# Sinkhorn attention feeding an affine ResMLP on one core: bulk loads placed elsewhere, and the strided weight columns of v copied by GpSimd into tiles of their own

## The chip, the cores and the metric

The kernel runs on one core of one Trainium2 chip. The metric is the device time of one execution in microseconds (us), the median of several runs. A core has TensorE for matmuls (PE in the profile, with its weight loads shown apart as PEld), VectorE (DVE), ScalarE (ACT), GpSimd (POOL) and SyncE (SP). In this kernel SyncE only issues DMAs; GpSimd computes and also issues the DMAs that convert float32 inputs to 16 bits on their way into the core.

## What is computed

The first half is attention over 8 blocks of 96 rows whose keys and values are mixed across blocks by a matrix P, made from `sort_net` by five rounds of exponential, row and column normalisation. The second half is a token mix and a two-layer channel MLP.

```python
# q, k, v: (4, 8, 768, 64); sort_net: (4, 8, 8, 8)
for _ in range(5):
    P = exp(P - max(P, -1)); P = P / (sum(P, -1) + 1e-9); P = P / (sum(P, -2) + 1e-9)
k_sorted, v_sorted = einsum('bhij,bhjcd->bhicd', P, k_b), einsum('bhij,bhjcd->bhicd', P, v_b)
attn = softmax(0.125 * q_b @ k_sorted.T)          # inside each of the 8 blocks of 96
x = (attn @ v_sorted)                              # -> (4, 768, 512), heads side by side
a1 = alpha1 * x + beta1
u = x + lam * einsum('ts,bsd->btd', w_tok, a1)     # w_tok (768, 768)
out = u + lam * (relu((alpha2 * u + beta2) @ w_ch1) @ w_ch2)   # 512 -> 2048 -> 512
```

## The kernel before, in words

The four batches pass through attention, then through a bounce to DRAM that turns the layout round, then through the MLP. The order of the instructions on each engine is the order in which the program is written; the program interleaves generators by hand, and there is no scheduler.

The opening, in order: GpSimd issues the loads of q and k of batch 0, v of batches 0 and 1 (one tile, `raw`), k of batch 1, the token matrix `wt16`, and three broadcasts of `lam`, `alpha1` and `beta1` over 128 partitions (L156 to L158). `sinkhorn(0)` makes P for batches 0 and 1 (L192 to L212). `mix_k01(0)` mixes the keys of batch 0 on TensorE (L277), and ScalarE and VectorE evict each psum tile, half each (`evict_k`, L259 and L261), into two tiles `kT`. Then GpSimd issues `load_q(1)`, all of W1 and W2 and half of the second v load (L142, L668, L670, L128).

`scores_max(0)` (matmuls L399, row maxima L405 on VectorE) runs interleaved with `mix_v01` (L319), which mixes the values of batches 0 and 1. Its weights are columns of `raw` seen as (t, d): the 96 elements of one column stand 64 elements apart. ScalarE evicts most of it (L327).

`heads(0)` runs softmax and values of batch 0 in eight steps (`scores` L443 and L451, exponential L458, `values` L468, scaled L478). After steps 3 and 7, `bounce` writes a half of x to DRAM in six DMAs and reads it back in one (L491, L493, on the SyncE queue); the result is `x16`, in halves g = 0 and 1. Six sums of rows of `wt16` (`row_sum`, L619 on VectorE and L622 on ScalarE) stand between the steps. GpSimd then makes `rb` from them (L696, six instructions) and `add_x(0)` adds `rb` to x (L515), so `u` is started.

While x travels, TensorE transposes `wt16` (`tok_weights`, L607), mixes the keys of batch 1 (`mix_k01(1)`) and transposes q of batch 1 (`q_path(1)`, L366). GpSimd issues the second k load and `load_q(2)` behind `add_x(0)`.

From there two generators are interleaved by credits: `mixing` (token mix `tok_mix`, L525, with L531 on VectorE, the addition L532 on GpSimd and the cast L533 on ScalarE; transposes `u_transposes` L542; channel layers `ch1` L571 and `ch2` L590) and `attention` for the batches 1 to 3. `sinkhorn(1)` is advanced one step at each part of `mixing`. The attention ends long before `mixing` does; the end of the program is the channel layers of batch 3.

Of the kernel before, what the change touches and what calls it, by code (L numbers as in the profile page):

```python
# [19 lines left out]
def kernel(  # L20
# [18 lines left out]
    nc = tc.nc  # L39
# [110 lines left out]
    load_k01(1)  # L150
    wt16 = moep.tile([128, NT, S], F16, name="wt16", tag="u", bufs=2)
    nc.gpsimd.dma_start(wt16[:], moe_w_tok.rearrange("(k p) s -> p k s", p=128))
    lamB = wt([128, C], FT, "lamB")
    b1lB = mt([128, C], FT, "tmp", 2)
    a1lB = wt([128, C], FT, "a1lB")
    nc.gpsimd.dma_start(lamB[:], moe_lam.partition_broadcast(128))  # L156
    nc.gpsimd.dma_start(a1lB[:], moe_alpha1.partition_broadcast(128))
    nc.gpsimd.dma_start(b1lB[:], moe_beta1.partition_broadcast(128))  # L158
# [28 lines left out]
    def sinkhorn(bp):  # L187
# [59 lines left out]
    def kT_tiles(b):  # L247

        for h2 in range(2):
            kT_of[b, h2] = at([128, 16, BLK], F16, "kT", 4)  # L250

    def evict_k(b, ps, cols, t16):
        for h2 in range(2):
            dst = kT_of[b, h2][:, :, t16 * 16:(t16 + 1) * 16].rearrange(
                "p c (b t) -> p c b t", b=2
            )
            src = cols[:, h2 * 16:h2 * 16 + 16]
            if h2 == 0:
                nc.scalar.copy(dst, src)  # L259
            else:  # L260
                nc.vector.tensor_copy(dst, src)  # L261

    def mix_k01(b, pools):
        raw = raw_of["k", 0]
        kT_tiles(b)
        for t16 in range(BLK // 16):
# [15 lines left out]
            evict_k(b, ps, ps[:, :, 0:256].rearrange("p b (t c) -> p c b t", c=32), t16)  # L282
            yield

    def mix_k23(P, pools):
        raw = raw_of["k", 1]
        for b in (2, 3):
            kT_tiles(b)
        for t16 in range(BLK // 16):
# [13 lines left out]
            for b2 in range(2):  # L303
                evict_k(2 + b2, ps, cols[:, b2 * 32:b2 * 32 + 32], t16)
# [8 lines left out]
    def mix_v01(pool):  # L313

        raw = raw_of["v", 0][:].rearrange("p (t d) -> p d t", d=D)
        for d8 in range(D // 8):
            ps = ps2(pool)
            for dd in range(8):
                nc.tensor.matmul(  # L319
                    ps[0:BLK, dd // 4, (dd % 4) * 128:(dd % 4 + 1) * 128],  # L320
                    raw[:, d8 * 8 + dd, :], PV[:], start=True, stop=True,
                )
# [66 lines left out]
    def scores_max(b):  # L389

        mx = at([BLK, 2, H4, NB], FT, "mx", 1)
        for n in range(2 * H4):
            h4, g = divmod(n, 2)
            sp = ps2(psS)
            for i1 in range(4):
                i = g * 4 + i1
                for hl in range(2):
# [4 lines left out]
                        kT_of[b, h4 // 2][r, h4 % 2 * 8 + i, :],  # L402
# [29 lines left out]
    def heads(b, xpool):  # L432
# [5 lines left out]
        def scores(n):  # L438
# [8 lines left out]
            for i1 in range(4):  # L447
                i = g * 4 + i1
                for hl in range(2):
# [3 lines left out]
                        kT_of[b, h4 // 2][r, h4 % 2 * 8 + i, :],  # L453
# [56 lines left out]
    def add_x(b):  # L510
        u_of[b] = mt([128, NT, C], FT, "u", 2)
        for g in range(2):
            for k0, kn in ((0, 2), (2, 1)):
                kt = slice(g * 3 + k0, g * 3 + k0 + kn)
                nc.gpsimd.tensor_tensor(  # L515
                    u_of[b][:, kt], x16_of[b, g][:, k0:k0 + kn], rb[:, kt], ALU.add
                )
# [18 lines left out]
    def u_transposes(b, half):  # L536
        for c2 in range(2):
            ps = psS.tile([128, 2, 1024], BF, name="uT_ps", tag="psS")
# [127 lines left out]
    load_q(1)  # L666
    for ci in range(CT):
        nc.gpsimd.dma_start(W1[:, ci, :], moe_w_ch1[ci * 128:(ci + 1) * 128, :])  # L668
# [120 lines left out]
```

## Time and profile before

| | |
|---|---|
| median of 3 runs | 355.72 us (353.84 to 356.33) |
| profiled execution: its own time, its span | 356.3 us, 354.5 us |
| TensorE busy, weight loads busy | 310.7 us (88%), 187.7 us |
| VectorE, ScalarE, GpSimd busy | 157.0, 123.1, 117.1 us |
| mean granted TensorE clock | 0.968 |
| first matmul of `tok_mix(0)`, first matmul of `ch1` | 68.03 us, 99.08 us |
| last matmul of attention's last stage to the end | 231.7 to 354.5 us: channel layers and token mixes alone |

The span runs from the first to the last instruction. Times inside it are counted from its start. Busy shares are means over stages with different limits: TensorE is busy for nearly all of the time after about 100 us, and has holes before.

### The profile page before, as it was taken

How to read it: one execution, taken by the hardware profiler on the slowest of the kernel's cores; microseconds unless marked ns; L12 is line 12 of the kernel's file. 1: busy time of each engine (PE TensorE's matmuls, PEld its weight loads, DVE VectorE, ACT ScalarE, POOL GpSimd, SP SyncE). 2: the span in 40 equal slices, each digit the busy share in tenths (PEclk: the TensorE clock that was granted, in tenths of full speed). 3: DMA queues.
4: the chain of work that ended last, by engine and by line, in shares of the span. 5: the costliest groups of instructions: out<-in, count | busy, mean ns of one | idle time of the engine just before them, and what ended most of it. 6: DMA issues, size and time to landing. Idle time of an engine off the chain costs nothing.

```text
span 354.5 us, 6763 instructions
## 1 busy us (share of the span) xinstructions
PE 310.7 (88%) x2878; PEld 187.7 (53%) x2878; DVE 157.0 (44%) x298; ACT 123.1 (35%) x204; POOL 117.1 (33%) x113
## 2 busy tenths in 40 slices
PE   1869998666578889999889989999999999999994
PEld 1768888422245544654455645664554554554541
DVE  4355474235654444559644583434311134213223
ACT  3225564202334522642443503533331225240310
POOL 8223573385200011836311001718211657300000
PEclk9999999986868999999999999999999999999998
DMA  7999999549000233697014401301410200100101
GB/s 95 220 203 251 214 211 232 162 90 185 3 0 2 46 84 109 229 152 98 11 59 112 91 2 59 77 2 41 137 46 1 91 0 0 61 30 31 59 16 73
DMA packets 33325, 31.76 MB, mean 90 GB/s; under 512 B 15696, under 2 KB 28752, under 8 KB 32784
## 3 DMA queue, kind: packets, MB, share of 16 engines
q0 software_dynamic: 8912, 15.60, 23.7%
q1 hardware_dynamic: 24384, 15.75, 17.7%
q8 instruction: 22, 0.36, 0.4%
q14 instruction: 7, 0.06, 0.0%
HBM read 35.14 MB, written 11.01 MB: 130 GB/s over the span
## 4 chain that ended last, share of the span: by engine, by line
PE 78%; DVE 6%; ACT 5%; DMA 4%; issue 3%; POOL 2%; SPq 1%; DVEq 0%; ACTq 0%; POOLq 0%
PE psM L571 25%; PE psM L590 23%; PE psM L525 8%; PE psM L319 3%; PE psS L399 3%; PE psS L468 3%; PE psS L443 3%; DMA xscr<-xnat 3%; ACT ET L458 3%; PE psS L451 2%; PE uT_ps L542 2%; PE q_ps L366 1%; PE psM L468 1%; PE psS L297 1%; DVE mx L405 1%
## 5 line engine op out<-in xcount | busy, mean ns | idle before, releaser
L571 PE MATMUL psM<-a2T,W 128*128 128x384 bf16 x512 | 91.6, 334 | 0.0
L590 PE MATMUL psM<-W,hT 128*128 128x512 bf16 x384 | 87.4, 379 | 0.0
L571 PEld LDWEIGHTS <-W 128*128 128x128 bf16 x512 | 49.2, 100 | 32.8 <-issue 2.7
L599 POOL TENSOR_TENSOR u<-u,tmp 128x512 f32<-128x512 f32 x18 | 22.8, 1268 | 124.4 <-DVE tmp L597 67.7
L581 ACT ACTIVATE hT<-psM 128x768 bf16<-128x768 f32 x48 | 38.9, 811 | 70.9 <-PE psM L571 70.9
L590 PEld LDWEIGHTS <-hT 128*128 128x128 bf16 x384 | 36.5, 98 | 41.0
L525 PE MATMUL psM<-x,w_tokT 128*128 128x512 f16 x144 | 37.9, 415 | 2.4 <-DMA x<-xscr 2.4
L532 POOL TENSOR_TENSOR u<-u,tmp 128x512 f32<-128x512 f32 x24 | 30.4, 1272 | 25.1 <-DVE tmp L531 20.9
L458 ACT ACTIVATE ET<-psS 96x768 f16<-96x768 f32 x32 | 25.5, 803 | 35.6 <-PE psS L451 35.6
L597 DVE TENSOR_TENSOR tmp<-psM,lamB 128x512 f32<-128x512 f32 x24 | 16.6, 691 | 47.0 <-PE psM L590 46.1
L579 DVE TENSOR_SCALAR hT<-psM 128x768 bf16<-128x768 f32 x16 | 15.3, 957 | 41.6 <-PE psM L571 41.6
L405 DVE TENSOR_REDUCE mx<-psS 96x8 f32<-96x768 f32 x32 | 29.9, 947 | 7.2 <-PE psS L399 7.1
L533 ACT CAST u<-u 128x512 bf16<-128x512 f32 x24 | 14.8, 618 | 48.2 <-POOL u L532 48.2
L515 POOL TENSOR_TENSOR u<-x,rb 128x1024 f32<-128x1024 f16 (+1 forms) x16 | 25.7, 1638 | 12.0 <-DMA x<-xscr 12.0
L525 PEld LDWEIGHTS <-w_tokT 128*128 128x128 f16 x144 | 13.9, 104 | 19.6 <-issue 6.7
L531 DVE TENSOR_TENSOR tmp<-psM,a1lB 128x512 f32<-128x512 f32 x24 | 16.6, 690 | 14.4 <-PE psM L525 14.4
L468 PEld LDWEIGHTS <-ET 96*96 96x96 f16 x256 | 16.4, 140 | 6.0 <-ACT ET L458 2.1
L201 PE MATMUL psS<-sortP,blk 128*128 128x8 f32 x20 | 4.6, 304 | 14.4 <-DVE sortP L198 9.3
L142 POOL DMA_DIRECT2D qn<-in_q_dram x16 | 11.6, 739 | 16.3 <-DMA raw<-in_v_dram 6.7
L478 DVE TENSOR_TENSOR xnat<-psS,recip 96x512 f16<-96x512 f32 x24 | 16.5, 686 | 1.2 <-DVE recip L477 0.3
L399 PEld LDWEIGHTS <-qT 64*96 64x96 f16 x256 | 10.2, 147 | 11.4 <-issue 9.3
L399 PE MATMUL psS<-kT,qT 64*96 64x96 f16 x256 | 13.6, 242 | 2.9 <-DVE mx L405 1.5
(96 smaller groups left out, 310.8 us busy)
## 6 DMA issues: line engine op xcount, KB each, us to landing
out_dram<-u SPq DMA_DIRECT2D x24, 256.0 KB, 2.0
W<-in_moe_w_ch_dram POOLq DMA_DIRECT2D x8, 512.0 KB, 14.3
qn<-in_q_dram POOLq DMA_DIRECT2D x16, 192.0 KB, 8.2
raw<-in_k_dram POOLq DMA_DIRECT2D x8, 384.0 KB, 8.2
xscr<-xnat SPq DMA_DIRECT2D x48, 64.0 KB, 2.2
x<-xscr SPq DMA_DIRECT2D x8, 384.0 KB, 3.3
raw<-in_v_dram POOLq DMA_DIRECT2D x1, 1536.0 KB, 16.2
raw<-in_v_dram POOLq DMA_DIRECT2D x4, 384.0 KB, 20.3
```

Of the source, the lines that this page charges most:

```text
L399: nc.tensor.matmul(sp[0:BLK, hl, i1 * BLK:(i1 + 1) * BLK], qT_of[b, h4][r, i * BLK:(i + 1) * BLK], kT_of[b, h4 // 2][r, h4 % 2 * 8 + i, :] ...
L405: nc.vector.tensor_reduce(mx[:, :, h4, g * 4:(g + 1) * 4], sp[0:BLK, :, 0:4 * BLK].rearrange("p l (i t) -> p l i t", t=BLK), AXX, ALU.max,)
L458: nc.scalar.activation(ET[:].rearrange("p l i s -> p l (i s)"), sp[0:BLK, :, 0:4 * BLK], AF.Exp, scale=scale,)
L468: nc.tensor.matmul(xp[0:BLK, hl, i1 * VP:i1 * VP + D + 1], ETs[n][:, hl, i1, :], vS[:, (hl * H4 + h4) * 8 + g * 4 + i1, 0:D + 1], start=Tr ...
L515: nc.gpsimd.tensor_tensor(u_of[b][:, kt], x16_of[b, g][:, k0:k0 + kn], rb[:, kt], ALU.add)
L525: nc.tensor.matmul(ps[:, 0, :], w_tokT[ks][:, kt * 128:(kt + 1) * 128], x16_of[b, ks // 3][:, ks % 3, :], start=(ks == 0), stop=(ks == NT ...
L531: nc.vector.tensor_tensor(tmp[:], ps[:, 0, :], a1lB[:], ALU.mult)
L532: nc.gpsimd.tensor_tensor(u[:, kt], u[:, kt], tmp[:], ALU.add)
L571: nc.tensor.matmul(ps[:, m1, 0:384], W1[:, ci, m * 128:(m + 1) * 128], a2T_of[b, half, ci][:], start=(ci == 0), stop=(ci == CT - 1),)
L581: nc.scalar.activation(t_[:], ps[:, :, 0:384], AF.Relu)
L590: nc.tensor.matmul(ps[:, 0, :], hT[m // 2][:, m % 2, k1 * 128:(k1 + 1) * 128], W2[:, m, :], start=(m == 0), stop=(m == HT - 1),)
L599: eng.tensor_tensor(u[:, kt], u[:, kt], tmp[:], ALU.add)
```

## The change

GpSimd's load order is another: `wt16` comes before k of batch 1, q of batch 1 is issued at the start, only half of W1 is issued before the value mix, the other half after the first half of `add_x(0)`, W2 after its second half, and the second loads of v and k and `load_q(2)` after `tok_mix(0)`. `lam`, `alpha1` and `beta1` are loaded by SyncE into one partition, multiplied there and spread by GpSimd's `partition_broadcast`; the built program has a reload of GpSimd's instruction library before the first of these and another before the first `rb`. `gather` copies eight columns of v at a time (128 x 8 x 96, 16 bits) into a contiguous tile on GpSimd, two ahead of the matmuls that take their weights from it. Each key eviction is one instruction, on ScalarE and VectorE in turn. All row sums are VectorE's and stand beside the value mix. `tok_weights` and `mix_k01(1)` each carry six steps of `sinkhorn(1)`, and `q_path(1)` moves into the interleaved attention. The first row maximum of a Sinkhorn run enters the exponential as a bias. The first `u_transposes` uses the other psum pool.

```diff
...
     load_q(0)
     load_k01(0)
     load_v0()
-    load_k01(1)
     wt16 = moep.tile([128, NT, S], F16, name="wt16", tag="u", bufs=2)
     nc.gpsimd.dma_start(wt16[:], moe_w_tok.rearrange("(k p) s -> p k s", p=128))
+    load_k01(1)
+    load_q(1)
+
+
+    rows = moep.tile([1, 3, C], FT, name="rows", tag="u16", bufs=1)
+    for n, src in enumerate((moe_lam, moe_alpha1, moe_beta1)):
+        nc.sync.dma_start(rows[:, n, :], src.unsqueeze(0))
     lamB = wt([128, C], FT, "lamB")
+    a1lB = wt([128, C], FT, "a1lB")
     b1lB = mt([128, C], FT, "tmp", 2)
-    a1lB = wt([128, C], FT, "a1lB")
-    nc.gpsimd.dma_start(lamB[:], moe_lam.partition_broadcast(128))
-    nc.gpsimd.dma_start(a1lB[:], moe_alpha1.partition_broadcast(128))
-    nc.gpsimd.dma_start(b1lB[:], moe_beta1.partition_broadcast(128))
+    for n in (1, 2):
+        nc.gpsimd.tensor_tensor(rows[:, n, :], rows[:, n, :], rows[:, 0, :], ALU.mult)
+    for n, t_ in enumerate((lamB, a1lB, b1lB)):
+        nc.gpsimd.partition_broadcast(t_[:], rows[:, n, :])
 
     w_tokT = [wt([128, S], F16, f"w_tokT_{i}") for i in range(NT)]
     W1 = wt([128, CT, HID], BF, "W1")
...
         rs = wt([128, 1], FT, f"rs{bp}")
         c8 = wt([128, NB], FT, f"c8{bp}")
 
-        nc.vector.tensor_reduce(rs[:], P[:], AXX, ALU.max)
-        nc.vector.tensor_scalar(P[:], P[:], rs[:], None, op0=ALU.subtract)
+        top = wt([128, 1], FT, f"top{bp}")
+        nc.vector.tensor_reduce(top[:], P[:], AXX, ALU.max, negate=True)
         for it in range(5):
-            nc.scalar.activation(P[:], P[:], AF.Exp, accum_out=rs[:])
+            if it == 0:
+                nc.scalar.activation(P[:], P[:], AF.Exp, bias=top[:], accum_out=rs[:])
+            else:
+                nc.scalar.activation(P[:], P[:], AF.Exp, accum_out=rs[:])
             yield
             nc.vector.reciprocal(rs[:], rs[:])
             nc.vector.tensor_scalar(P[:], P[:], rs[:], None, op0=ALU.mult)
...
 
     kT_of, vS_of = {}, {}
 
-    def kT_tiles(b):
-
-        for h2 in range(2):
-            kT_of[b, h2] = at([128, 16, BLK], F16, "kT", 4)
-
-    def evict_k(b, ps, cols, t16):
-        for h2 in range(2):
-            dst = kT_of[b, h2][:, :, t16 * 16:(t16 + 1) * 16].rearrange(
-                "p c (b t) -> p c b t", b=2
-            )
-            src = cols[:, h2 * 16:h2 * 16 + 16]
-            if h2 == 0:
-                nc.scalar.copy(dst, src)
-            else:
-                nc.vector.tensor_copy(dst, src)
+    def kT_tile(b):
+
+        kT_of[b] = at([128, H4 * NB, BLK], F16, "kT", 2)
+
+    def evict_k(b, cols, t16):
+        dst = kT_of[b][:, :, t16 * 16:(t16 + 1) * 16].rearrange("p c (b t) -> p c b t", b=2)
+        if t16 % 2 == 0:
+            nc.scalar.copy(dst, cols)
+        else:
+            nc.vector.tensor_copy(dst, cols)
 
     def mix_k01(b, pools):
         raw = raw_of["k", 0]
-        kT_tiles(b)
+        kT_tile(b)
         for t16 in range(BLK // 16):
             ps = ps2(pools[t16 % len(pools)])
             for turn in range(2):
...
     def mix_v01(pool):
 
         raw = raw_of["v", 0][:].rearrange("p (t d) -> p d t", d=D)
+        cols = {}
+
+        def gather(d8):
+            cols[d8] = moep.tile([128, 8, BLK], F16, name="vcol", tag="hT", bufs=11)
+            nc.gpsimd.tensor_copy(cols[d8][:], raw[:, d8 * 8:(d8 + 1) * 8, :])
+
+        gather(0)
+        gather(1)
         for d8 in range(D // 8):
+            if d8 + 2 < D // 8:
+                gather(d8 + 2)
             ps = ps2(pool)
             for dd in range(8):
                 nc.tensor.matmul(
                     ps[0:BLK, dd // 4, (dd % 4) * 128:(dd % 4 + 1) * 128],
-                    raw[:, d8 * 8 + dd, :], PV[:], start=True, stop=True,
+                    cols[d8][:, dd, :], PV[:], start=True, stop=True,
                 )
             for b in range(2):
                 dst = vS_of[b][:, :, d8 * 8:(d8 + 1) * 8].rearrange("p c (b d) -> p c b d", b=2)
...
 
     u_of, u16_of, a2T_of = {}, {}, {}
 
-    def add_x(b):
-        u_of[b] = mt([128, NT, C], FT, "u", 2)
-        for g in range(2):
-            for k0, kn in ((0, 2), (2, 1)):
-                kt = slice(g * 3 + k0, g * 3 + k0 + kn)
-                nc.gpsimd.tensor_tensor(
-                    u_of[b][:, kt], x16_of[b, g][:, k0:k0 + kn], rb[:, kt], ALU.add
-                )
+    def add_x(b, g):
+        if g == 0:
+            u_of[b] = mt([128, NT, C], FT, "u", 2)
+        for k0, kn in ((0, 2), (2, 1)):
+            kt = slice(g * 3 + k0, g * 3 + k0 + kn)
+            nc.gpsimd.tensor_tensor(
+                u_of[b][:, kt], x16_of[b, g][:, k0:k0 + kn], rb[:, kt], ALU.add
+            )
 
     def tok_mix(b):
         u = u_of[b]
...
             yield
 
     def row_sum(tt):
-        if tt % 2:
-            nc.vector.tensor_reduce(rowsum[:, tt:tt + 1], wt16[:, tt, :], AXX, ALU.add)
-        else:
-            junk = mt([128, 2, 384], BF, "hT", 11)
-            nc.scalar.activation(
-                junk[:].rearrange("p a c -> p (a c)"), wt16[:, tt, :], AF.Identity,
-                accum_out=rowsum[:, tt:tt + 1],
-            )
+        nc.vector.tensor_reduce(rowsum[:, tt:tt + 1], wt16[:, tt, :], AXX, ALU.add)
+
+    def load_w1(ci):
+        nc.gpsimd.dma_start(W1[:, ci, :], moe_w_ch1[ci * 128:(ci + 1) * 128, :])
 
     def run(gen, n=None):
         while n is None or n > 0:
...
         run(mix, 1)
     run(mix)
 
-    load_q(1)
-    for ci in range(CT):
-        nc.gpsimd.dma_start(W1[:, ci, :], moe_w_ch1[ci * 128:(ci + 1) * 128, :])
+    for ci in range(CT // 2):
+        load_w1(ci)
+    top, mix = scores_max(0), mix_v01(psM)
+    run(top, 3)
+    for n in range(5):
+        run(mix, 1)
+        run(top, 1)
+        if n > 1:
+            row_sum(n - 2)
+    run(mix, 1)
+    run(top, 1)
+    row_sum(3)
+    run(mix, 1)
+    run(top)
+    row_sum(4)
+    run(mix)
+
+    att0 = heads(0, psM)
+    run(att0, 2)
+    row_sum(5)
+    run(att0)
+    for tt in range(NT):
+        nc.gpsimd.tensor_scalar(rb[:, tt, :], b1lB[:], rowsum[:, tt:tt + 1], None, op0=ALU.mult)
+    add_x(0, 0)
+    for ci in range(CT // 2, CT):
+        load_w1(ci)
+    add_x(0, 1)
     for m4_ in range(4):
         nc.gpsimd.dma_start(
             W2[:, m4_ * 4:(m4_ + 1) * 4, :],
             moe_w_ch2[m4_ * 512:(m4_ + 1) * 512, :].rearrange("(m p) c -> p m c", p=128),
         )
-    nc.gpsimd.tensor_tensor(a1lB[:], a1lB[:], lamB[:], ALU.mult)
-    nc.gpsimd.tensor_tensor(b1lB[:], b1lB[:], lamB[:], ALU.mult)
-    load_23("v", v)
-
-    top, mix = scores_max(0), mix_v01(psM)
-    run(top, 3)
-    for n in range(5):
-        run(mix, 1)
-        run(top, 1)
-    run(mix, 1)
-    run(top, 1)
-    run(mix, 1)
-    run(top)
-    run(mix)
-
-    att0 = heads(0, psM)
-    run(att0, 1)
-    for n in range(2 * H4):
-        run(att0, 1)
-        if 0 < n < NT + 1:
-            row_sum(n - 1)
-    for kt in range(NT):
-        nc.gpsimd.tensor_scalar(rb[:, kt, :], b1lB[:], rowsum[:, kt:kt + 1], None, op0=ALU.mult)
-    add_x(0)
-    run(tok_weights())
-    run(mix_k01(1, [psS, psM]))
-    run(q_path(1, psS))
-    load_23("k", k)
-    load_q(2)
-
-
     sink = sinkhorn(1)
+    for part in tok_weights():
+        run(sink, 1)
+    for part in mix_k01(1, [psS, psM]):
+        run(sink, 1)
+
 
     def attention():
+        yield from q_path(1, psS)
         yield from scores_max(1)
         yield from heads(1, psS)
         run(sink)
...
     def mixing():
 
         yield from tok_mix(0)
-        u_transposes(0, 0)
+        load_23("v", v)
+        load_23("k", k)
+        load_q(2)
+        u_transposes(0, 0, psM)
         yield 2.0
         for b in range(B):
             part = ch1(b, 0)
             yield next(part)
             yield next(part)
             if b == 0:
-                u_transposes(0, 1)
+                u_transposes(0, 1, psS)
             yield from part
             for k1 in range(3):
                 yield from ch2(b, 0, k1)
             if b + 1 < B:
-                add_x(b + 1)
+                for g in range(2):
+                    add_x(b + 1, g)
             yield from ch1(b, 1)
             if b + 1 < B:
                 yield from tok_mix(b + 1)
             for k1 in range(3):
                 yield from ch2(b, 1, k1)
                 if b + 1 < B and k1 < 2:
-                    u_transposes(b + 1, k1)
+                    u_transposes(b + 1, k1, psS)
                     yield 0.5
 
     att_ = attention()
...
```

The scores' matmuls read `kT_of[b][r, h4 * 8 + i, :]` in place of `kT_of[b, h4 // 2][r, h4 % 2 * 8 + i, :]`: one tile of keys for a batch in place of two.

More of the change, by code (lines that the diff above doesn't have):

```diff
@@ L281, in mix_k01 @@
                         )
-            evict_k(b, ps, ps[:, :, 0:256].rearrange("p b (t c) -> p c b t", c=32), t16)
+            evict_k(b, ps[:, :, 0:256].rearrange("p b (t c) -> p c b t", c=32), t16)
             yield
@@ L287, in mix_k23 @@
         for b in (2, 3):
-            kT_tiles(b)
+            kT_tile(b)
         for t16 in range(BLK // 16):
@@ L303, in mix_k23 @@
             for b2 in range(2):
-                evict_k(2 + b2, ps, cols[:, b2 * 32:b2 * 32 + 32], t16)
+                evict_k(2 + b2, cols[:, b2 * 32:b2 * 32 + 32], t16)
             yield 1.2
@@ L401, in scores_max @@
                         qT_of[b, h4][r, i * BLK:(i + 1) * BLK],
-                        kT_of[b, h4 // 2][r, h4 % 2 * 8 + i, :],
+                        kT_of[b][r, h4 * 8 + i, :],
                         start=True, stop=True,
@@ L452, in scores @@
                         sp[0:BLK, hl, i1 * BLK:(i1 + 1) * BLK],
-                        kT_of[b, h4 // 2][r, h4 % 2 * 8 + i, :],
+                        kT_of[b][r, h4 * 8 + i, :],
                         qT_of[b, h4][r, i * BLK:(i + 1) * BLK],
@@ L534, in tok_mix, with u_transposes @@
             yield 1.0
-    def u_transposes(b, half):
+    def u_transposes(b, half, pool):
         for c2 in range(2):
-            ps = psS.tile([128, 2, 1024], BF, name="uT_ps", tag="psS")
+            ps = pool.tile(
+                [128, 2, 1024], BF, name="uT_ps", tag="psS" if pool is psS else "psM"
+            )
             for c1 in range(2):
```

## The prediction

> **What bounds the kernel now.** The page's slices come first, to find where TensorE is not yet the limit.
>
> ```profile
> PE   1869998666578889999889989999999999999994
> DMA  7999999549000233697014401301410200100101
> ```
>
> A slice is 8.9 us. From about 100 us on TensorE is full and attention's work only fills in between the channel layers, so what the opening gains or loses is carried to the end. TensorE is thin in slices 7 to 10, about 60 to 95 us; the DMA engines are full until 65 us. The chain in order of time says what that stretch waits for:
>
> ```profile
> 59.34 8.96 DMA xscr<-xnat
> ...
> 68.50 3.19 DMA x<-xscr
> ...
> 74.99 0.87 POOL raw L128 x2
> ...
> 77.02 2.84 POOL qn L142 x4
> 79.86 1.31 POOL u L532
> ```
>
> The last half of x of batch 0 takes 8.96 us to be written, against the page's median of 2.2 us for these 64 KB DMAs. Then GpSimd issues eight loads (74.99 to 79.86) ahead of its first L532, and the token mix waits. The windows show why the write is slow (length, then busy time and count of PE, PEld, DVE, ACT, POOL, clock, DMA share, GB/s):
>
> ```profile
> 55.00:60.00 5.00, 4.91 (x101) 4.39 (x101) 2.10 (x4) 2.05 (x4) 1.57 (x2) 1.00 1.18 234
> 60.00:65.00 5.00, 3.36 (x128) 3.21 (x126) 1.70 (x4) 1.43 (x5) 0.00 (x0) 1.00 0.96 227
> ```
>
> W1, W2 and v, issued from 30.84 to 46.76, fill the engines. TensorE's timeline shows the price:
>
> ```profile
> 71.73 0.81 PE L525 MATMUL psM<-x,w_tokT 128*128 128x512 f16 x3 [2.39 <-DMA x<-xscr]
> ...
> 72.96 2.74 PE L525 MATMUL psM<-x,w_tokT 128*128 128x512 f16 x6
> ...
> 76.03 1.47 PE L525 MATMUL psM<-x,w_tokT 128*128 128x512 f16 x6
> 82.58 0.45 PE L201 MATMUL psS<-sortP,blk 128*128 128x8 f32 x2 [5.07 <-issue]
> ```
>
> A wait of 2.39 us for x, a hole of 5.07 us behind GpSimd, and the same six matmuls in 2.74 or 1.47 us, at two clock rates. `ch1` begins at 99.1 us. The sum below is for that moment.
>
> **When the gathers can start.** The built order of GpSimd is now: loads of q, k, v, `wt16`, k and q of batch 1; two products; library reload; three broadcasts; two W1 issues; eight gathers; reload; six `rb`; `add_x(0, 0)`; two W1; `add_x(0, 1)`; four W2; six L532. Each load waits for the one eight before it, so the second W1 issue waits for `wt16`, and all gathers stand behind it. GpSimd's timeline of before gives the landings:
>
> ```profile
> 21.98 0.73 POOL L142 DMA_DIRECT2D qn<-in_q_dram  x1 [6.74 <-DMA raw<-in_v_dram]
> ...
> 25.14 0.71 POOL L142 DMA_DIRECT2D qn<-in_q_dram  x1 [0.70 <-DMA raw<-in_k_dram]
> ...
> 30.84 1.82 POOL L668 DMA_DIRECT2D W<-in_moe_w_ch_dram  x3 [4.99 <-DMA wt<-in_moe_w_tok_dram]
> ```
>
> v lands at 22.0, k at 25.1, `wt16` 5.7 us behind k. Moved ahead of k it lands at 27.7, so no gather begins before 28.2. The q issues end at 16.6 (the third waits for the transposes of q, done at 15.2); products 2 x 1.27 (row of L675) bring 19.2. A reload has no row. Below it is bounded by the reload of before, which fits between the Memset that ends at 0.92 and the affine select at 1.00: 0.1. [...] Broadcasts have no row either: between 0.1 and 2.1 each (L515), taken as a 128x512 float32 product, 1.27: 30.6. Two issues of 0.53: the first gather at 31.7.
>
> **The gathers.** Three forms bound a copy of 768 elements:
>
> ```profile
> L515 POOL TENSOR_TENSOR u<-x,rb 128x1024 f32<-128x1024 f16 x8 | 17.0, 2122 | 12.0 <-DMA x<-xscr 12.0
> ...
> L319 PEld LDWEIGHTS <-raw 128*96 128x96 f16 x64 | 11.0, 256 | 0.5
> L696 POOL TENSOR_SCALAR rb<-tmp,rowsum 128x512 bf16<-128x512 f32 x6 | 9.3, 1559 | 0.0
> L515 POOL TENSOR_TENSOR u<-x,rb 128x512 f32<-128x512 f16 x8 | 9.2, 1154 | 0.0
> ```
>
> The two L515 forms give 1.89 ns an element and 0.19 fixed: 1.64. With one input at half the slope: 0.91. L696, which has one input, gives 3.04 ns: 2.34; and if strided reads cost what the same columns cost TensorE (256 ns against 140 for the contiguous 96 columns of L468), 1.83 times as much: 4.3. I take 1.64, the row that reads 16 bits. Eight make 13.1: gathers end at 44.8. [...]
>
> TensorE's part falls from 1.50 (the spacing of L319's eights) to 8 x 0.12 (L607's rate), 0.96. That would be 4.3 us less, but the gathers pace the stage at 1.64, so none of it is gained. The last part ends at 45.8, and `heads(0)` starts then instead of 39.4: **6.4 us later**.
>
> **From heads to the channel layer.** `heads(0)` took 13.15 (39.40 to 52.55), of which a row sum of ScalarE held the chain for 0.8; without it the end is at 58.2. `tok_weights` 5.4 and `mix_k01(1)` 6.9 follow as before, with four Sinkhorn matmul pairs of 0.57 between: 72.8. x must be there by then: last scaled output 1.6 after the heads, 59.8; six issues 2.8, landing 2.2, read 0.4 + 3.3: 68.5, hidden by 4.3. GpSimd: 44.8, reload 2.2 (64 KB through quiet engines), `rb` 9.3: 56.3; the first x half comes at 63.8 (54.2 + 3.6 + 2.2 + 3.7); `add_x` 3.2, W1 1.1, wait to 68.5, `add_x` 3.2, W2 3.0: free at 74.7, while the first L531 ends at 76.2. Hidden by 1.5.
>
> `tok_mix(0)` took 19.7 (71.73 to 91.43), less the hole 14.6. Four q parts of 0.75 come in and two score parts of 0.5 go out, one group more runs at 1.47: 15.3, so 88.1. Then L531 0.69, L532 1.27, cast 0.62 and two `a2T` 1.24 in line on ScalarE: `ch1` at 92.0, **7.1 before 99.1**. Later, four score parts that stood ahead of `ch1` stand behind it (4 x 0.25 at the fast rate, +1.0), and four Sinkhorn pairs are already done (4 x 0.28, -1.1): 0.
>
> **Edits at nothing.** The row sums (6 x 0.94 on VectorE) lie beside the gathers; uncovered, 5.6. The shorter Sinkhorn start (L193, 0.43) is hidden by k, landing at 14.5. A key eviction of 512 elements takes ScalarE 0.59 (L327) and VectorE 0.68 (L329) in place of 0.37 and 0.42 at once: 0.3 later for the first scores, and beside `ch1` hidden by its matmuls; uncovered, 12 x 0.3. Loads of v, k, q for later batches are issued from about 89 (7 us of GpSimd, with waits for W2 and v); the next work there is the first L599, after 120, and v is wanted at about 124. W1's second half, 1 MB at 230 GB/s, lands near 73, wanted at 92.
>
> **The sum.** Span 354.5 - 7.1 = 347.4. The profiled execution took 356.3 (1.8 around its span), 0.6 over the median of 355.72; from the median, 348.6.
>
> **Rivals.** *The gathers keep up* (0.17): start 28.2, copies 0.91; then TensorE's 0.96 + 0.48 paces, and heads begin near 40.6: 5.2 less, 343.4; 340.4 if `ch1` also starts at the fast clock (its first three eights took 2.67, 2.01 and 2.30, not 1.30: 3.0). For it: one input only. Against: the stride and the reload. *The gathers eat the gain* (0.13): L696's 2.34 adds 8 x 0.70: 354.2. *GpSimd becomes the bound* (0.10), on the slower side: 4.3 a copy ends the gathers at 66.1, 21.3 later than I have it: 369.9. The gain is gone from 2.53 a copy, and from 2.97 it is over 1% slower. For it: TensorE's own strided loads; against: L515's rate. *x is no faster* (0.03): the write still takes 8.96, 6.8 more less the 4.3 cover: 351.1. The slices speak against it, since nothing else would load then.
>
> **Numbers.** The forecast has 0.57, own range 345 to 352. About 1% (3.6 us) is what this measurement tells from no change. Faster: 0.57 + 0.17 + 0.03 = 0.77; same 0.13; slower 0.10. The range runs from the quickest rival to a little over the third: 340.4 to 355.5.
>
> **What would show it.** Gathers starting near 31.7 at 1.64; first L443 near 45.8; x writes at 2.2; no `[... <-DMA x<-xscr]` on TensorE; no hole in `tok_mix(0)`; `ch1` at 92. Wrong if a copy takes over 2.5, a reload is much over 9, or the stretch after `ch1` is no longer 255 us.

## The result, and the profile after

The changed kernel took 350.61 us (median; 349.38 to 351.70) beside 355.72 for the kernel before, each over four executions: ratio 0.9864, with a 95% interval of 0.9814 to 0.9914. The forecast was 348.6: 5.1 us were gained where 7.1 were forecast. The profiled execution took 349.38 us over a span of 347.6; the forecast span was 347.4. That closeness flatters the forecast: the two profiled executions lie 6.9 us apart and the medians 5.1, since the profiled one of the changed kernel was the quickest of its four and that of the kernel before the slowest of its four. The question is whether the sum was right too. The page of the changed kernel, with TensorE, GpSimd, granted clock and DMA in 40 slices of 8.7 us (counted from 0 below):

```profile
PE   2844599797699989996989998999999999999994
...
POOL 8419747833730118084011013607211757300000
PEclk9999855568899999999699999999999999999998
DMA  7999405796399455991004400303300100101101
```

From 35 to 60 us (slices 4 to 6) the DMA engines now have 4, 0 and 5 tenths and are full no longer. TensorE's thin slices 7 to 11 have filled up (7, 9, 7, 6, 9); in exchange slices 2 to 4, 17 to 43 us, show only 4, 4 and 5. GpSimd's timeline (start, length of the group, engine, line, operation, then in brackets the idle time before it and what ended that):

```profile
26.26 0.80 POOL L165 PARTITION_BROADCAST lamB<-rows  x1 [7.33 <-issue]
...
28.24 1.30 POOL L638 DMA_DIRECT2D W<-in_moe_w_ch_dram  x2
29.52 11.47 POOL L325 COPY vcol<-raw 128x768 f16<-128x768 f16 x8
48.24 9.28 POOL L701 TENSOR_SCALAR rb<-tmp,rowsum 128x512 bf16<-128x512 f32 x6 [7.26 <-issue]
59.69 3.23 POOL L530 TENSOR_TENSOR u<-x,rb 128x1024 f32<-128x1024 f16 x2 [2.17 <-DMA x<-xscr]
```

Both library reloads show as idle time with no releaser, 7.33 and 7.26. The eight gathers run from 29.52 to 41.0, 1.43 apart. GpSimd now waits for x; TensorE no longer does.

TensorE's timeline from the value mix (L334) to the first channel layer (L588):

```profile
31.05 1.09 PE L334 MATMUL psM<-PV,vcol 128*96 128x128 f16 x8 [6.69 <-POOL vcol L325]
...
36.74 0.65 PE L334 MATMUL psM<-PV,vcol 128*96 128x128 f16 x8 [0.46 <-POOL vcol L325]
...
43.27 0.56 PE L458 MATMUL psS<-Dt,nsel 64*96 64x384 bf16 x2 [1.00 <-DVE Dt L439]
...
67.75 0.57 PE L211 MATMUL psS<-sortP,blk 128*128 128x8 f32 x2 [1.49 <-DVE sortP L208]
...
71.64 2.72 PE L540 MATMUL psM<-x,w_tokT 128*128 128x512 f16 x6
...
81.02 0.53 PE L381 MATMUL q_ps<-ident,qn 128*64 128x128 f16 x12 [0.87 <-ACT qT L390]
...
93.71 1.76 PE L588 MATMUL psM<-a2T,W 128*128 128x384 bf16 x5 [1.88 <-ACT a2T L568]
```

TensorE waits 6.69 us for the first gather, not at all for the next three, and 0.46 to 0.78 us for each of the three behind them. `heads(0)` starts at 43.27, behind VectorE (`Dt`, L439) and not behind a gather. The token mix starts at 71.64 without a wait for x.

Five markers of a profile are compared below: the start of `heads(0)`, of `tok_mix(0)`, of `ch1`, of `tok_mix(1)` and of `tok_mix(2)`. Two executions of the changed kernel (this one and `a1_after_again`) differ by 1.6 to 2.1 us from the first marker on; 1.2 of that is the first reload, which took 7.33 us in the one and 8.57 in the other. So a difference under 2 us between two profiles' markers is not read as an effect; stretches between markers repeat better.

| kernel | heads | tok_mix(0) | ch1 | tok_mix(1) | tok_mix(2) | span |
|---|---|---|---|---|---|---|
| before | 39.4 | 68.0 | 99.1 | 158.2 | 238.1 | 354.5 |
| changed | 43.3 | 71.6 | 93.7 | 146.8 | 231.4 | 347.6 |
| a1_after_again | 45.0 | 73.4 | 95.4 | 148.6 | 233.4 | 349.7 |
| a2_no_gather | 40.3 | 68.3 | 89.0 | 143.6 | 225.3 | 341.6 |
| a4_hold_only | 39.6 | 66.5 | 89.5 | 149.0 | 228.9 | 345.3 |
| b3_hold_gather | 35.1 | 61.0 | 84.6 | 141.8 | 221.7 | 338.1 |
| b4_hold_psm_late | 39.6 | 66.4 | 80.9 | 147.1 | 227.0 | 343.4 |
| c1_gather_sinks | 39.2 | 66.0 | 81.0 | 133.9 | 213.8 | 330.2 |

At `ch1` the change has gained 5.4 us in this execution, 3.7 in a1. After `ch1` it gains 1.5 more, out of two larger parts that nearly cancel: from `ch1` to `tok_mix(1)` 53.1 instead of 59.1, from `tok_mix(1)` to `tok_mix(2)` 84.6 instead of 79.9.

### The profile page after: what moved, and what is told of

It is laid out like the page before. It is cut to its first block, busy times and chain, and to the rows that moved or that the text cites. A ratio compares the mean times of both kernels' runs of the same rounds, so it can differ in the third digit from the quotient of the medians.

```text
span 347.6 us, 6762 instructions
## 1 busy us (share of the span) xinstructions
PE 303.9 (87%) x2878; PEld 179.7 (52%) x2878; DVE 158.6 (46%) x287; ACT 119.0 (34%) x186; POOL 129.0 (37%) x121
## 4 chain that ended last, share of the span: by engine, by line
PE 78%; DVE 10%; issue 4%; POOL 3%; ACT 3%; DVEq 0%; ACTq 0%; POOLq 0%
PE psM L588 25%; PE psM L607 25%; PE psM L540 9%; PE psS L458 3%; PE psS L483 3%; PE psS L466 2%; PE psS L414 2%; PE q_ps L381 2%; PE psM L483 2%; DVE mx L420 2%; PE psS L211 2%; ACT ET L473 1%; PE uT_ps L559 1%; DVE sortP L208 1%; PE psS L302 1%
## 5 line engine op out<-in xcount | busy, mean ns | idle before, releaser
L588 PE MATMUL psM<-a2T,W 128*128 128x384 bf16 x512 | 90.2, 329 | 2.3 <-ACT a2T L568 1.9
L607 PE MATMUL psM<-W,hT 128*128 128x512 bf16 x384 | 89.6, 386 | 0.0
L588 PEld LDWEIGHTS <-W 128*128 128x128 bf16 x512 | 48.6, 99 | 34.1 <-issue 3.6
L607 PEld LDWEIGHTS <-hT 128*128 128x128 bf16 x384 | 36.8, 99 | 42.1 <-issue 2.4
L547 POOL TENSOR_TENSOR u<-u,tmp 128x512 f32<-128x512 f32 x24 | 30.3, 1272 | 39.2 <-DVE tmp L546 33.5
L420 DVE TENSOR_REDUCE mx<-psS 96x8 f32<-96x768 f32 x32 | 29.8, 947 | 14.2 <-PE psS L414 14.1
L540 PE MATMUL psM<-x,w_tokT 128*128 128x512 f16 x144 | 36.1, 402 | 0.0
L596 DVE TENSOR_SCALAR hT<-psM 128x768 bf16<-128x768 f32 x16 | 15.3, 957 | 41.6 <-PE psM L588 41.6
L530 POOL TENSOR_TENSOR u<-x,rb 128x1024 f32<-128x1024 f16 (+1 forms) x16 | 25.7, 1633 | 3.5 <-DMA x<-xscr 3.5
L546 DVE TENSOR_TENSOR tmp<-psM,a1lB 128x512 f32<-128x512 f32 x24 | 16.5, 688 | 13.9 <-PE psM L540 12.9
L483 PEld LDWEIGHTS <-ET 96*96 96x96 f16 x256 | 16.4, 141 | 3.1 <-ACT ET L473 0.7
L458 PE MATMUL psS<-Dt,nsel 64*96 64x384 bf16 x64 | 13.4, 409 | 4.2 <-DVE Dt L439 2.3
L211 PE MATMUL psS<-sortP,blk 128*128 128x8 f32 x20 | 5.7, 357 | 11.7 <-DVE sortP L208 11.7
L492 DVE RECIPROCAL recip<-psS 96x8 f32<-96x8 f32 x24 | 4.9, 204 | 23.4 <-PE psS L483 23.4
```

What stands on the lines that cost most here:

```text
L420: nc.vector.tensor_reduce(mx[:, :, h4, g * 4:(g + 1) * 4], sp[0:BLK, :, 0:4 * BLK].rearrange("p l (i t) -> p l i t", t=BLK), AXX, ALU.max,)
L458: nc.tensor.matmul(sp[0:BLK, hl, 0:4 * BLK], nsel[r, h4, :], D_of[b, g][r], start=True, stop=False, skip_group_check=True,)
L483: nc.tensor.matmul(xp[0:BLK, hl, i1 * VP:i1 * VP + D + 1], ETs[n][:, hl, i1, :], vS[:, (hl * H4 + h4) * 8 + g * 4 + i1, 0:D + 1], start=Tr ...
L530: nc.gpsimd.tensor_tensor(u_of[b][:, kt], x16_of[b, g][:, k0:k0 + kn], rb[:, kt], ALU.add)
L540: nc.tensor.matmul(ps[:, 0, :], w_tokT[ks][:, kt * 128:(kt + 1) * 128], x16_of[b, ks // 3][:, ks % 3, :], start=(ks == 0), stop=(ks == NT ...
L547: nc.gpsimd.tensor_tensor(u[:, kt], u[:, kt], tmp[:], ALU.add)
```

## The experiments

Each median stands with its ratio to the kernel before and the 95% interval; the kernel before took 355.01, 354.45 and 356.45 us beside the groups a, b and c.

### Group a: the parts of the change

**a1_after_again** is the changed kernel, repeated.

> The changed kernel once more, as the mark for the others of this group. Both theories: ratio to before near 0.986, span 347 to 350 us, first ch1 matmul near 93.7 us.

Measured: 350.26 us, 0.9866 (0.9834 to 0.9898).

**a2_no_gather** takes the gathers out of the changed kernel.

```diff
-        gather(0)
-        gather(1)
         for d8 in range(D // 8):
-            if d8 + 2 < D // 8:
-                gather(d8 + 2)
...
-                    cols[d8][:, dd, :], PV[:], start=True, stop=True,
+                    raw[:, d8 * 8 + dd, :], PV[:], start=True, stop=True,
```

> The changed kernel with the value mix taking its weights from the strided columns again. Theory (the opening is a sum along x's path, and the gathers are a price in it): the value mix starts near 24.4 us instead of 31.05, its eight parts of 1.50 + 0.48 end near 40, heads start near 40.5 instead of 43.3, ch1 near 91, time about 2.8 us less than the changed kernel. Rival (the contiguous weights are what gains): heads start no earlier, time 3 us or more above the changed kernel.

Measured: 345.38 us, 0.972 (0.9685 to 0.9754). Without the gathers the kernel is 4.9 us quicker than a1. In its timeline the value mix starts at 25.56, 5.5 and 7.2 us earlier than in the two profiles with gathers, at the slower pace of strided weights (1.57 us for the first eight matmuls, 0.65 to 1.09 from the gathered tiles):

```profile
25.56 1.57 PE L324 MATMUL psM<-PV,raw 128*96 128x128 f16 x8
...
27.54 1.57 PE L324 MATMUL psM<-PV,raw 128*96 128x128 f16 x8
...
40.25 0.55 PE L448 MATMUL psS<-Dt,nsel 64*96 64x384 bf16 x2 [0.45 <-DVE Dt L429]
```

The gathers do quicken the parts they feed: a weight load takes 153 ns from the gathered tiles, 256 from `raw`. They lose more by being late: as placed, the gathers cost the kernel about 5 us.

**a3_pe_broadcast** makes the three broadcasts on TensorE and ScalarE, so that no reload is needed.

```diff
-    for n, t_ in enumerate((lamB, a1lB, b1lB)):
-        nc.gpsimd.partition_broadcast(t_[:], rows[:, n, :])
...
+        for n, t_ in part:
+            nc.tensor.matmul(ps[:, n % 2, :], ones1[:], rows[:, n, :], start=True, stop=True)
+            nc.scalar.copy(t_[:], ps[:, n % 2, :])
```

> The changed kernel with the three broadcasts made by TensorE (a row of ones times the row) and copied by ScalarE, so that GpSimd reloads no library. Theory: the gaps of 7.3 us at 18.9 and 41.0 on GpSimd go; the gathers then wait for wt16 alone and start near 28.2 instead of 29.5, rb ends 8 us earlier but was not on the path; time 1.3 us less than the changed kernel. Rival (the reloads are on the path in full): 7 us less.

Measured: 351.08 us, 0.9888 (0.9856 to 0.9921): no gain. The gathers start at 27.83, against 29.52 and 31.18 in the two profiles of the changed kernel, and no earlier because the second W1 issue ahead of them waits for `wt16`. The float32 matmuls of the broadcast then hold TensorE for 3.75 us, so that the value mix starts at 31.64 (31.05 and 32.72 in the changed kernel):

```profile
27.29 0.54 POOL L638 DMA_DIRECT2D W<-in_moe_w_ch_dram  x1 [5.07 <-DMA wt<-in_moe_w_tok_dram]
```

```profile
27.96 3.75 PE L686 MATMUL psM<-rows,ones 1*128 1x512 f32 x4 [0.77 <-ACT lamB L687]
31.64 1.09 PE L334 MATMUL psM<-PV,vcol 128*96 128x128 f16 x8
```

So the run doesn't price the reload alone. It does show that the reload is only one of two things ahead of the gathers: with it gone, they still wait 5.07 us for `wt16`.

**a4_hold_only** is the kernel before with nothing but the order of the loads changed.

```diff
-    load_k01(1)
     wt16 = moep.tile([128, NT, S], F16, name="wt16", tag="u", bufs=2)
     nc.gpsimd.dma_start(wt16[:], moe_w_tok.rearrange("(k p) s -> p k s", p=128))
+    load_k01(1)
...
-    for ci in range(CT):
+    for ci in range(CT // 2):
...
-    load_23("v", v)
...
-    add_x(0)
+    add_x(0, (0,))
+    for ci in range(CT // 2, CT):
+        load_w1(ci)
+    add_x(0, (1,))
+    for m4_ in range(4):
...
-    load_23("k", k)
-    load_q(2)
...
         yield from tok_mix(0)
+        load_23("v", v)
+        load_23("k", k)
+        load_q(2)
```

> The kernel before with nothing but the order of GpSimd's loads changed as in the change (wt16 ahead of k of batch 1, half of W1 early, the rest of W1 and W2 around add_x, v, k and q of later batches after the first token mix). Theory: heads still start at 39.4, x writes take about 2.2 us, x is there by 63, token mix starts at 68.0 without a wait and without the 5 us hole, ch1 near 91, time about 347, below the changed kernel. Rival (the gain needs the gathers or the new interleaving): time 352 or more.

Measured: 346.24 us, 0.974 (0.9699 to 0.9781). The order of the loads alone gives 8.8 us, more than the whole change gives (4.8 in a1, same group). Its `heads(0)` starts where that of the kernel before does; the 9.6 us at `ch1` are all won after it.

### Group b: where the loads and the gathers stand

**b1_loads_early** issues the second half of W1, W2 and the second v load of the changed kernel ahead of `heads(0)` again, so that x travels beside them.

```diff
+    for ci in range(CT // 2, CT):
+        load_w1(ci)
+    for m4_ in range(4):
...
+    load_23("v", v)
     att0 = heads(0, psM)
...
     add_x(0, 0)
-    for ci in range(CT // 2, CT):
-        load_w1(ci)
     add_x(0, 1)
-    for m4_ in range(4):
...
         yield from tok_mix(0)
-        load_23("v", v)
         load_23("k", k)
```

> The changed kernel with the second half of W1, all of W2 and the second load of v issued right behind the gathers, before the heads, so that they travel while x does. Theory (holding back is what brings x in time): the x writes take 7 to 9 us again, the second half of x comes near 75 instead of 65.5, past the cover of tok_weights and mix_k01(1), ch1 some 3 to 4 us later, time 353 to 354. Rival (with 15 us of other work on TensorE behind the heads, x is hidden either way): 350.3, as the changed kernel.

Measured: 350.86 us, 0.9881 (0.9848 to 0.9914), as the changed kernel. The writes of x are slow again (median 7.1 us against 2.3 us in the changed kernel), and TensorE waits for x again:

```profile
75.33 1.44 PE L540 MATMUL psM<-x,w_tokT 128*128 128x512 f16 x3 [2.40 <-DMA x<-xscr]
```

Yet `ch1` starts at 95.6, and at 95.4 in a1. From `heads(0)` to `ch1` it is 51.5 us instead of 50.4, so the wait of 2.40 is made up only in part: the way to the token mix is 1.0 shorter, and the groups of six behind the wait are quicker (the fourth and fifth take 1.47 each, 2.61 and 1.72 in the changed kernel). The next two stretches make up the rest (52.8 and 83.5 us, against 53.1 and 84.6). Holding W1, W2 and v back is worth nothing in the changed kernel. GpSimd is idle for long before its first `rb`:

```profile
62.57 9.28 POOL L709 TENSOR_SCALAR rb<-tmp,rowsum 128x512 bf16<-128x512 f32 x6 [12.34 <-DVE sortP L219]
```

The Sinkhorn step named there stands later in the program and can't be what `rb` waited for, and the row sums had long been done; what is left is the second reload, here beside DMA engines at 9 tenths or more throughout.

**b2_rowsum_heads** moves the row sums back between the steps of `heads(0)`, still on VectorE.

```diff
-        if n > 1:
-            row_sum(n - 2)
...
-    run(att0, 2)
-    row_sum(5)
+    run(att0, 1)
+    for n in range(2 * H4):
+        run(att0, 1)
+        if 0 < n < NT + 1:
+            row_sum(n - 1)
     run(att0)
```

> The changed kernel with the row sums, still on VectorE, put between the steps of heads(0) as before. Theory (row sums stand in the chain between the row maxima, so they and not the last gather start the heads): heads start 1.2 to 2 us earlier, time 348.5 to 349. Rival (the gathers pace the stage alone): 350.3, as the changed kernel.

Measured: 351.08 us, 0.9881 (0.9848 to 0.9915): no gain. `heads(0)` starts 1.4 us after the last gather instead of 2.3, but the sums now alternate with the scaled outputs on VectorE, as the chain in order of time shows:

```profile
39.79 2.32 DVE mh L430
...
50.34 0.86 DVE rowsum L635
...
51.35 0.69 DVE xnat L493
52.04 0.86 DVE rowsum L635
```

The first line shows why the heads could not start earlier still: the copy of the row maxima (`mh`) starts at 39.79 beside the gathers, takes 2.32 us and ends with the last of them, at 42.1; in the changed kernel it starts at 40.62 and takes 0.42.

**b3_hold_gather** adds the eight gathers to a4, placed right behind the landing of v and ahead of every later load. There are no reloads in it.

```diff
+    raw_d = raw_of["v", 0][:].rearrange("p (t d) -> p d t", d=D)
+    vcol_of = {}
+    for d8 in range(D // 8):
+        vcol_of[d8] = moep.tile([128, 8, BLK], F16, name="vcol", tag="hT", bufs=11)
+        nc.gpsimd.tensor_copy(vcol_of[d8][:], raw_d[:, d8 * 8:(d8 + 1) * 8, :])
+
     load_q(1)
```

> The kernel with nothing but the load order changed (346.2 in the group before), and all eight gathers on GpSimd where v lands, ahead of every issue that waits for later loads, with no library reload. Theory (the gathers lose by where they stand, not by what they are): gathers from 22 to 33.5 at 1.43 each, value mix parts of 1.0 + 0.5, heads start near 36 instead of 39.9, time 342 to 343. Rival (a gather costs as much as it saves wherever it stands): 346 or more.

Measured: 340.48 us, 0.9594 (0.956 to 0.9628), 5.8 us under a4 by the medians and 5.2 by the ratios. GpSimd's timeline:

```profile
21.61 11.51 POOL L670 COPY vcol<-raw 128x768 f16<-128x768 f16 x8 [8.48 <-DMA raw<-in_v_dram]
```

The same eight copies at the same length start 7.9 us earlier, and `heads(0)` at 35.1 instead of 39.6. So gathering is a gain; its place in GpSimd's queue turned it into a loss.

**b4_hold_psm_late** is a4 with the first `u_transposes` in the other psum pool, and `sinkhorn(1)` stepped only from the eighth part of `mixing` on.

```diff
-        u_transposes(0, 0)
+        u_transposes(0, 0, psM)
...
-    for part in mixing():
-        run(sink, 1)
+    for n, part in enumerate(mixing()):
+        if n > 6:
+            run(sink, 1)
```

> The kernel with nothing but the load order changed, with the first u_transposes in the other psum pool (as in the change) and with sinkhorn(1) beginning only at the eighth part of mixing, so that none of its steps stands in tok_mix(0). Theory (what is left between 66 and 89 us there is waits: VectorE and ScalarE in order behind Sinkhorn steps, 2.6 us, and the psum pool, 3 to 4 us): tok_mix(0) takes 11 to 12 instead of 14.2, ch1 near 83 instead of 89.5, time 340. Rival (GpSimd's L532 sets that pace whatever stands between): 345 to 346.

Measured: 345.48 us, 0.9751 (0.971 to 0.9791), no better than a4, although `ch1` starts 8.6 us earlier (80.9). From `ch1` to `tok_mix(1)` it needs 66.2 instead of 59.6: the Sinkhorn steps, needed by batches 2 and 3, only moved. TensorE's timeline has waits of 2.40 and 1.30 us for `sortP` near 115 us, where a4 has none. The run makes two edits at once and doesn't price them apart. An earlier `ch1` is not by itself an earlier end.

### Group c: the Sinkhorn steps, and GpSimd's queue

**c1_gather_sinks** is b3 with `sinkhorn(1)` stepped beside `sinkhorn(0)` at the very start.

```diff
-    run(sink, 2)
+    both(2)
     nc.scalar.copy(ident16[:], ident32[:])
-    run(sink, 3)
+    both(3)
...
     PK, PV = big_p0()
+    run(other)
...
-    sink = sinkhorn(1)
+    sink = other
```

(`both(n)` advances `sinkhorn(0)` and `sinkhorn(1)` in turn, n times.)

> The kernel with the load order changed and the gathers where v lands (340.5), with all of sinkhorn(1) run step by step beside sinkhorn(0) in the first 15 us. Theory (Sinkhorn steps inside tok_mix(0) and ch1 hold TensorE, as the 59 us from the first ch1 to the second token mix before and 53 after say): tok_mix(0) loses its hole of 3 us, that stretch falls from 57 to 53, the start costs 1 us: 334 to 335. Rival (the order of attention paces those stretches, and what is gained there is given back by the third token mix): 339 to 341.

Measured: 332.04 us, 0.9317 (0.9292 to 0.9342), 8.4 us under b3 by the medians and 9.8 by the ratios, more than expected. The opening is later by 4.1 at `heads(0)`, but `tok_mix(0)` has no hole left and takes 10.1 us:

```profile
66.03 1.60 PE L525 MATMUL psM<-x,w_tokT 128*128 128x512 f16 x6
...
74.71 1.47 PE L525 MATMUL psM<-x,w_tokT 128*128 128x512 f16 x6
```

**c2_gather_sinks_psm** is c1 with the first `u_transposes` in the other psum pool, as in the change.

```diff
-        u_transposes(0, 0)
+        u_transposes(0, 0, psM)
```

> The same, and the first u_transposes in the other psum pool as in the change. Theory: 3 us less between tok_mix(0) and ch1, 331 to 332. Rival (the start of ch1 is no longer what is carried to the end): as the one without it.

Measured: 331.13 us, 0.93 (0.9272 to 0.9328), the quickest kernel of this study: 19 us under the changed kernel, 25 under the one before. The pool is worth 0.9 us by the medians, less than expected, and the two intervals overlap, so even that is not clear of the noise.

**c3_sink_in_mixing** is the changed kernel with `sinkhorn(1)` left to `mixing`, where the kernel before has it.

```diff
-    for part in tok_weights():
-        run(sink, 1)
-    for part in mix_k01(1, [psS, psM]):
-        run(sink, 1)
+    run(tok_weights())
+    run(mix_k01(1, [psS, psM]))
```

> The changed kernel with sinkhorn(1) left to the parts of mixing as before, not beside tok_weights and mix_k01(1). Theory: the token mix starts 3 us earlier, near 69, but the stretch from the first ch1 to the second token mix is 58 to 59 instead of 53: 352. Rival (the steps ahead of the token mix are only a cost): 347 to 348.

Measured: 350.76 us, 0.9864 (0.9826 to 0.9902), no difference from the change. Its profiled execution took 3.9 us more than its median, so only its own stretches are read. From heads to token mix it needs 23.0 (28.4 in the changed kernel), from there to `ch1` 24.3 (22.1), from `ch1` to `tok_mix(1)` 59.5 (53.1). By the medians the steps cost about the same in either place; of the places tried, only the opening of c1 takes them cheaply.

**c4_kq_behind** is the kernel before with only the second k load and `load_q(2)` moved behind `tok_mix(0)`. W1, W2 and v stay early.

```diff
-    load_23("k", k)
-    load_q(2)
-
-
     sink = sinkhorn(1)
...
         yield from tok_mix(0)
+        load_23("k", k)
+        load_q(2)
```

> The kernel before with the second k load and load_q(2) issued behind tok_mix(0), and all else as it was. Theory (the 5 us hole behind GpSimd's issues and the slow clock after it are the larger part of what the load order gives): x still late, token mix resumes near 71.7, no hole, ch1 near 93, 349 to 350. Rival (x's late landing is the larger part): 353 to 354.

Measured: 349.91 us, 0.9809 (0.9772 to 0.9845): 6.5 of the 8.8 us that the whole load order gives. TensorE still waits for x, but the hole of 5.07 us is gone, the five groups of six matmuls behind the wait take 1.47 us each, and `ch1` starts at 91.6:

```profile
70.88 0.81 PE L525 MATMUL psM<-x,w_tokT 128*128 128x512 f16 x3 [1.25 <-DMA x<-xscr]
...
76.84 0.36 PE L201 MATMUL psS<-sortP,blk 128*128 128x8 f32 x2 [1.73 <-issue]
...
91.62 2.74 PE L571 MATMUL psM<-a2T,W 128*128 128x384 bf16 x8
```

So most of what the load order gives comes from moving eight DMA issues from ahead of the first L532 to behind the token mix. The smaller part is all else in the order, x travelling alone among it; no run takes that apart.

## Why the prediction was right, and where it was not

The forecast was right in its direction and mechanism: the opening gets later because of the gathers, and the stage between x and `ch1` gets shorter by more. a2 and a4 show both halves apart. Step by step the sum held partly because errors cancel, which is luck: `heads(0)` started 2.5 us earlier than forecast, and the four terms behind it (heads, way to the token mix, token mix, way to `ch1`) came out 0.8, 0.6, 2.0 and 0.9 larger.

**The gathers: mis-sized, on the safe side.** The first came at 29.52 (31.18 in a1; forecast 31.7), 1.43 apart (1.64), ending at 41.0 (44.8). The first reload came near its 7.6 (7.33, and 8.57 in a1), but by luck: 7.6 was the author's estimate, the median of the x writes before 100 us. No run shows that a reload has to do with such a write; the second took 7.26 in a stretch in which no DMA packet moved. The broadcasts were sized too large (0.67 apart against 1.27). The stride cost nothing like the upper bound of 4.3, taken from TensorE's strided loads: the copies took 1.49 each.

**"The row sums at nothing": wrong in the trace, harmless in the time.** The gathers end at 41.0, yet `heads(0)` starts at 43.27. The chain of the changed kernel in order of time, from 35 us on:

```profile
35.43 0.95 DVE mx L420
36.39 0.86 DVE rowsum L635
...
38.97 0.86 DVE mx L420
39.84 0.86 DVE rowsum L635
...
41.30 0.86 DVE rowsum L635
42.16 0.60 DVE vS L344
42.75 0.48 DVE Dt L439
```

Row sums and maxima alternate on VectorE with no gap; the maxima hold the mask matmul and so the heads. The row sums do not all lie beside the gathers: the one at 41.30 is on the path behind them. b2 shows that undoing it brings nothing, because between the heads they delay the scaled outputs in turn. A chain names what ended last, not what a removal is worth. The 0.8 us that ScalarE's row sums were to leave did not appear either: `heads(0)` took 13.1, not 12.35. The prediction also let the heads start as the last part of the value mix ends; that part ends at 42.27, and the heads wait 1.0 us more, for `Dt`.

**The second reload: wrong by 5 us, hidden.** It was put at 2.2, the time of a write of x through quiet DMA engines, which no run shows for a reload either. It took 7.26 (7.11 in a1) with the DMA engines idle (share 0.00 in that stretch), about as the first beside busy ones (7.33, share 1.12), so these two lengths do not follow the load on the engines. In b1 GpSimd was idle there for 12.34, beside engines at 9 tenths or more. GpSimd's additions still came in time, since x was there at 59.7 and 65.5 rather than 63.8 and 68.5.

**Heads to token mix: right, 15.2 against 14.6.** x was hidden, as said.

**`tok_mix(0)`: 17.3 against 15.3.** The stage was mis-sized by a wait that the prediction did not name. TensorE's own timeline of this stage has 2.2 us of waits (0.18, 0.46, 0.87 and 0.65). The largest, at 81.02, comes from the order on ScalarE: the q transposes wait for its copy of q (80.17), which stands behind its cast of `u` (79.65), which waits for GpSimd's addition at 78.36 to end (79.62). VectorE's and GpSimd's timelines show what follows:

```profile
78.38 1.26 DVE L208 TENSOR_SCALAR sortP<-sortP,rs 128x8 f32<-128x8 f32 x1
79.56 0.68 DVE L546 TENSOR_TENSOR tmp<-psM,a1lB 128x512 f32<-128x512 f32 x1
```

```profile
78.36 1.26 POOL L547 TENSOR_TENSOR u<-u,tmp 128x512 f32<-128x512 f32 x1 [1.75 <-DVE rs L207]
80.31 1.27 POOL L547 TENSOR_TENSOR u<-u,tmp 128x512 f32<-128x512 f32 x1 [0.70 <-DVE tmp L546]
```

A Sinkhorn step on 8 elements, 0.24 us in the median of its ten, takes 1.26 here and ends at 79.64, as GpSimd's addition beside it does at 79.62, and L546 stands behind it; the next addition waits for that. The two groups of six matmuls at the slow clock (2.72 and 2.61 us, granted 0.50 and 0.53) were in the forecast. The tail from the stage's end to `ch1` took 4.8, not 3.9. So `ch1` came at 93.7, not 92.0: a gain of 5.4, not 7.1.

**"The stretch after `ch1` stays 255 us": 253.9, but not because nothing happened.** The prediction's sentence that the opening's gain "is carried to the end" is not a rule: b4 gained 8.6 at `ch1` over a4 and kept nothing that the ratios show. In the changed kernel most Sinkhorn steps are done before the token mix (four of the five matmul pairs of L211), and `ch1` to `tok_mix(1)` is 6.0 shorter; c3, which puts them back, has 59.5 there again. The next batch gives 4.7 back, as TensorE's timeline of the changed kernel shows:

```profile
164.09 0.22 PE L434 MATMUL m_ps<-identbf,mh 96*128 96x96 bf16 x1 [2.25 <-DVE mh L431]
...
165.42 0.82 PE L559 MATMUL uT_ps<-identbf,u 128*128 128x128 bf16 x6 [0.78 <-DVE Dt L439]
166.04 3.62 PE L607 MATMUL psM<-W,hT 128*128 128x512 bf16 x8
...
170.39 2.39 PE L607 MATMUL psM<-W,hT 128*128 128x512 bf16 x8
...
176.72 1.89 PE L607 MATMUL psM<-W,hT 128*128 128x512 bf16 x8
```

After a wait of 2.25 us for VectorE, two groups run at a lower granted clock (0.50 and 0.79 at 166.04 and 170.39, 1.00 at 176.72): the 96 matmuls of this form take 24.99 us in this stretch against 22.74 before, 16 more q transposes take 0.6, 12 more score matmuls 0.7, and TensorE idles 0.9 more. All profiled kernels that are built on the one before have 79.9 in this stretch; those built on the change have 83 to 85, and a2 81.8. Whether the wait starts the slow stretch was not tested.

**The rivals.** *The gathers keep up* named the right direction for the copies and missed that VectorE then paces. *The gathers eat the gain* and *GpSimd becomes the bound* did not occur at 1.49 a copy, but a2 shows that the gathers do eat about half of what the load order gives. *x is no faster* did not occur: a write of x took 2.3 us (median of the twelve of batch 0).

What stays open: the price of a reload in time, since a3 changed TensorE's work as well; what in the change makes the stretch from `tok_mix(1)` to `tok_mix(2)` longer; and whether the psum pool is worth anything in c2.

## What to carry to other kernels

In a queue that both computes and issues DMAs in the order of the program, as GpSimd's here, place each operation by when its input lands: the same eight copies cost 5 us behind a library reload and a DMA issue that waits for a later load (from 29.52 us), and gained over 5 right behind the landing of v (from 21.61). Look at that queue for issues that stand ahead of an addition others wait for, before blaming the transfers themselves. A gain at the first dense stage has to be followed to the marker of the next batch: 8.6 us at `ch1` were worth nothing measurable at the end, where the work had only moved behind that marker.

## What the runs showed of the hardware

Where the built program has a reload of GpSimd's library, GpSimd was idle for 7.1 to 8.6 us: 7.33 and 8.57 at the first in two executions of the changed kernel, 8.57, 8.14 and 8.39 in a2, b1 and b2, beside busy DMA engines (share 1.12 in that of 7.33), and 7.26 and 7.11 at the second of the changed kernel, beside idle ones (0.00 in that of 7.26). At the second of a2 and of b1, with a share of 0.95 (from 30 to 40 us) and of 9 tenths or more, it was idle for 9.87 and 12.34 us. a3, which needs no reload, has none of these gaps.

A VectorE operation of 0.23 us took up to 1.35 us beside a GpSimd addition, and ended when that did. The answers for L208 in the changed kernel and for L198 in c1 (the same operation; ns min, median, max):

```profile
L208 DVE TENSOR_SCALAR sortP<-sortP,rs x10: 230/239/1353, 3.2 to 78.4; 128x8 f32<-128x8 f32 x10
```

```profile
L198 DVE TENSOR_SCALAR sortP<-sortP,rs x10: 230/230/267, 6.1 to 14.5; 128x8 f32<-128x8 f32 x10
```

The instance of 1.35 us starts at 66.25 and ends at 67.60; GpSimd's first L530 of that pair starts at 65.47 and takes 2.1 us, so it ends at about the same moment. It stands ahead of the wait of 1.49 us for `sortP` at 67.75 shown above. The reductions L420 keep their length beside such additions (0.94 us at 88.98, beside the addition from 89.14 to 90.40). b2's copy of 2.32 us, which ends with the gathers, is another case; what makes the two engines end together was not tested. It fits that Sinkhorn steps are cheap in c1, where these stand between 6.1 and 14.5 us, take 0.27 us at most, and GpSimd's first addition (L515) comes at 55.33; no run separates this from their other place in the queues.

The granted clock of the opening can't be read alone. The windows of 40 to 50 us of the kernel before and of 50 to 55 us of the changed kernel (length, busy time and count of PE, PEld, DVE, ACT and POOL, clock, DMA share, GB/s) lie in `heads(0)`:

```profile
40.00:50.00 10.00, 9.74 (x117) 8.11 (x115) 6.33 (x13) 7.07 (x12) 5.02 (x7) 1.00 1.14 208
```

```profile
50.00:55.00 5.00, 5.00 (x60) 4.18 (x60) 2.69 (x7) 2.68 (x4) 5.00 (x4) 0.50 0.35 58
```

The clock stands at 1.00 in the one and 0.50 in the other, yet the same eight value matmuls take 0.85 us in both (L468 and L483 of the two timelines). So the mean of 0.928 against 0.968 says nothing of slower work there.
